# Scores of two banks in one visit, and three rotating product banks, in a sliding-window attention block

## The chip, the cores and the metric

The kernel runs on one core of a Trainium2 chip. The metric is device time in microseconds (us) of one launch, lower is better. Times before are the median of three runs. One further execution was profiled, and every row below comes from its trace. PE is TensorE with its matrix multiplications, DVE is VectorE, ACT is ScalarE, POOL is GpSimd, SP is SyncE, which issues nearly all DMAs here. A "slot" below is the place ahead of one dense matmul.

## The reference

A transformer block on 2048 tokens of width 1024, in bfloat16: layer norm, attention with 32 heads of width 32 in which each query sees the 256 keys up to itself, a residual, a second layer norm, and a dense SiLU layer of width 3584 with a residual.

```python
qkv = (layernorm(x) @ wqkv).reshape(B, S, 3, 32, 32)
scores = einsum("bhqd,bhkd->bhqk", q, k) * 32 ** -0.5
mask = (idx[:, None] - idx[None, :] >= 0) & (idx[:, None] - idx[None, :] < 256)
p = softmax(where(mask, scores, -1e9))
h = x + einsum("bhqk,bhkd->bhqd", p, v).reshape(B, S, D) @ wo
out = h + silu(layernorm(h) @ w1) @ w2
```

## The kernel before

**Tiling.** Tokens go in `NB` = 4 blocks of 512, heads in `G` = 8 groups of four. Scores have the keys on the partitions and the queries along the row, so that their exponentials are used directly as weights of the product with the values; one extra column of ones in `v` (width `VW` = 33) gives the sum for the softmax. A score matmul contracts over 32 rows. Four heads sit on four row strips of the PE array and, where the keys are taken in halves of 64, two halves on two column strips: eight tiles stream at once.

**Dense work and what is put in between.** Attention is not a stage of its own. Dense matmuls of 512 columns come in groups of eight (`v_group`, `qk_group`, `wo_group`), each group into one bank of the eight that PE can write, which DVE then copies or adds out. Each dense matmul first calls `between`, and there `Stream.between` puts pieces of the attention of the block before. Block 0's attention lies between the projections of block 1, block 1's between those of block 2, block 2's between those of block 3, and block 3's between the first 24 groups of the output projection (`dense` list with `wo_group`). Each of these stretches has 192 dense matmuls. After them come the SiLU layers (`h1_group`, `mm2`), which take up the last pieces.

**Scores.** For blocks 1 to 3 each pair of groups has five bursts: one C burst (`scores_c`, the corner parts of both groups, 16 matmuls of 128 columns) and an X and a Y burst for each group (`scores_xy`, 24 matmuls of 320, 128 and 64 columns: 512 columns for each tile). A burst fills `sc[0]` and `sc[1]`, two tiles of two banks each, one bank a head. ACT then writes the exponentials into `c_ring` or a buffer of `xy_ring`: two instructions of 1024 elements after a C burst, and 768, 256, 768, 256 after an X or Y burst. POOL masks the triangles (`select`, four of 512 elements after an X or Y burst). Block 0 has two bursts a group (`scores_0`).

**Products.** `attn_out` multiplies the exponentials with the values: per group 16 outputs of three matmuls of 33 columns. The outputs of two heads fill a bank of `o_ps`; `o_ps[0]` and `o_ps[1]` take turns. `attn_norm` (DVE: reciprocal, then a multiply into `obuf`) follows each half of a group. After a group's second half `attn_transpose` is put on the list `late`, and SP issues it ahead of the next dense group. The pieces (`SPLIT`: 8, 8, 5, 6 and 5 outputs) run just before a burst, three bursts behind their own.

**Other queues.** DVE also has the layer norm steps of the next block (`ln1_steps`, `ln2_steps`): one step after a dense group, behind the group's own copy. In block 2's stretch these are four statistics steps (groups 1, 2, 4 and 5), four short ones and four normalizations. In the output-projection stretch the second layer norm's steps begin after group 11, and from group 14 on two follow each group.

**Banks.** Eight: `acc0` and `acc1` for dense groups, `o_ps0` and `o_ps1`, and four for `sc`. In the SiLU layers the four of `sc` become `hacc`, and six banks rotate.

Of the kernel before, what the change touches and what calls it, by code (L numbers as in the profile page):

```python
# [9 lines left out]
F32 = mybir.dt.float32  # L10
# [4 lines left out]
P = 128  # L15
# [25 lines left out]
SPLIT = [(0, 8), (8, 16), (16, 21), (21, 27), (27, 32)]  # L41
# [7 lines left out]
def kernel(  # L49
# [46 lines left out]
    o_ps = [ps.tile([P, 8, 64], F32, name=f"o_ps{i}") for i in range(2)]  # L96
    acc_ps = [ps.tile([P, 512], F32, name=f"acc{i}") for i in range(2)]
# [29 lines left out]
    xy_ring = [r_e[:, 3072 + 1280 * i:3072 + 1280 * (i + 1)] for i in range(8)]  # L127
# [46 lines left out]
    def busy(n):  # L174
        nc.tensor.matmul(o_ps[0][:].rearrange("p (a c) b -> p a (c b)", c=2)[:, 0:n], lhsT=warm, rhs=wide[:, 0:n], start=True, stop=True)
# [53 lines left out]
    acc_banks = list(a[:] for a in acc_ps)  # L229
# [50 lines left out]
    def chunk_of(i, bank, piece, pair, hh):  # L280
        if bank == "C":
            return c_ring[:, (i + 1) % 3, pair * 2 + hh, piece * P:(piece + 1) * P]
        if i < G:
            c0 = hh * 512 + piece * P
        else:
            c0 = 1024 + hh * P if piece == 2 else hh * 512 + (piece - piece // 3) * P
        return xy_ring[(i % 2 * 2 + "XY".index(bank)) * 2 + pair][:, c0:c0 + P]

    def scores_xy(b, g, odd):
        q0 = odd * P  # L290
        mid, first, last = odd, odd - 2, odd + 2

        parts = [
            (mid, 0, q0, q0 + 320, 64), (mid, 1, q0 + 64, q0 + 384, 128),
            (last, 0, q0 + 256, q0 + 384, 384), (first, 1, q0, q0 + 128, 0),
            (first, 0, q0, q0 + 64, 0), (last, 1, q0 + 320, q0 + 384, 448),
        ]
        for step in range(3):
            for hh in range(4):
                for kt, half, qa, qb, col in parts[step * 2:step * 2 + 2]:  # L300
                    r0 = hh * DH
                    t = b * 4 + kt
                    k0 = (t % 4) * P + half * 64
                    nc.tensor.matmul(  # L304
                        sc[hh // 2][half * 64:half * 64 + 64, hh % 2, col:col + qb - qa],
                        lhsT=kT[t // 4][r0:r0 + DH, g, k0:k0 + 64],
                        rhs=qT[b][r0:r0 + DH, g, qa:qb],
                        start=True, stop=True, tile_position=(r0, half * 64),
                    )
        for pair in range(2):  # L310
            e = xy_ring[((b * G + g) % 2 * 2 + odd) * 2 + pair]
            tri = e[:, 0:1024].rearrange("p (h c q) -> p h c q", h=2, q=256)
            bank = sc[pair]
            both = bank[:, :, 0:192]
            both = bass.AP(tensor=both.tensor, offset=both.offset, ap=[*both.ap[:2], [320, 2], both.ap[2]])
            nc.scalar.activation(out=tri[:, :, :, 64:256], in_=both, func=ACT.Exp, scale=scale)  # L316
            nc.scalar.activation(out=e[:, 1024:1280].rearrange("p (h q) -> p h q", q=P), in_=bank[:, :, 192:320], func=ACT.Exp, scale=scale)  # L317
            four = e[:, 0:1024].rearrange("p (c q) -> p c q", q=256)
            select(four[:, :, 0:P], four[:, :, 64:64 + P], False)
            select(four[:, :, P:2 * P], four[:, :, P:2 * P], True)  # L320

    def scores_c(b, g):
        s0, s1 = (b * G + g + 1) % 3, (b * G + g + 2) % 3
        order = (g, g + 1) if s0 < s1 else (g + 1, g)
        for n, gg in enumerate(order):
            for m, (kt, q) in enumerate(((-1, 0), (2, 3))):
                t = b * 4 + kt
                for hh in range(4):
                    r0 = hh * DH
                    nc.tensor.matmul(  # L330
                        sc[hh // 2][:, hh % 2, (n * 2 + m) * P:(n * 2 + m + 1) * P],
                        lhsT=kT[t // 4][r0:r0 + DH, gg, (t % 4) * P:(t % 4 + 1) * P],
                        rhs=qT[b][r0:r0 + DH, gg, q * P:(q + 1) * P],
                        start=True, stop=True, tile_position=(r0, 0),
                    )
        lo, hi = min(s0, s1), max(s0, s1)
        for pair in range(2):
            nc.scalar.activation(out=c_ring[:, lo:hi + 1:hi - lo, pair * 2:pair * 2 + 2, :],
                                 in_=sc[pair].rearrange("p h (n q) -> p n h q", q=256), func=ACT.Exp, scale=scale)

    def scores_0(g, odd):
# [9 lines left out]
        for step in range(0, len(parts), 2):  # L351
            for hh in range(4):
                for t, half, qa, qb, col in parts[step:step + 2]:
                    r0 = hh * DH
                    k0 = t * P + half * 64
                    nc.tensor.matmul(  # L356
                        sc[hh // 2][half * 64:half * 64 + 64, hh % 2, col:col + qb - qa],
                        lhsT=kT[0][r0:r0 + DH, g, k0:k0 + 64],
                        rhs=qT[0][r0:r0 + DH, g, qa:qb],
                        start=True, stop=True, tile_position=(r0, half * 64),  # L360
                    )
        for pair in range(2):
            e = xy_ring[(g % 2 * 2 + odd) * 2 + pair][:, 0:1024].rearrange("p (h q) -> p h q", q=512)
            nc.scalar.activation(out=e[:, :, 0:256], in_=sc[pair][:, :, 0:256], func=ACT.Exp, scale=scale)  # L364
            nc.scalar.activation(out=e[:, :, 320:512], in_=sc[pair][:, :, 256:448], func=ACT.Exp, scale=scale)
            nc.scalar.activation(out=c_ring[:, (g + 1) % 3, pair * 2:pair * 2 + 2, 128 + 64 * odd:192 + 64 * odd],
                                 in_=sc[pair][:, :, 448:512], func=ACT.Exp, scale=scale)
# [10 lines left out]
    def attn_out(b, g, first, last):  # L378
        i = b * G + g
        for n in range(first, last):  # L380
            pair, qt, hh = n // 8, n // 2 % 4, n % 2
            chunks = (CHUNKS if b else CHUNKS_0)[qt]
            for m, (kt, bank, piece) in enumerate(chunks):
                nc.tensor.matmul(  # L384
                    o_ps[pair][:, qt * 2 + hh, 0:VW],
                    lhsT=chunk_of(i, bank, piece, pair, hh),
# [6 lines left out]
    def attn_norm(i, pair):  # L393
        recip = small.tile([P, 8, 1], F32, name="recip", tag="recip")
        nc.vector.reciprocal(out=recip[:], in_=o_ps[pair][:, :, DH:VW])
        nc.vector.tensor_tensor(
            out=obuf[i % 3][:, :, pair * 64:(pair + 1) * 64].rearrange("p t (h d) -> p t h d", d=DH),
            in0=o_ps[pair][:, :, 0:DH].rearrange("p (t h) d -> p t h d", h=2),
# [8 lines left out]
    def attn_piece(b, g, first, last):  # L407

        for k in range(2):
            a, z = max(first - 16 * k, 0), min(last - 16 * k, 16)  # L410
            if a < z:
                attn_out(b, g + k, a, z)
                if z == 16:
                    late.append(lambda k=k: attn_transpose(b, g + k))

    class Stream:

        def __init__(self, b):  # L420
            self.bursts, self.pieces, self.done, self.seen = [], [], 0, 0
            self.behind = 3 if b else 2
            pending.extend(coming)
            coming.clear()
            for g in range(0, G, 2):
                if b:
                    self.bursts += [lambda g=g: scores_c(b, g)]
# [365 lines left out]
```

## Time and profile before

| | |
|---|---|
| median of three runs | 690.07 us (689.61 to 691.45) |
| the profiled execution | 689.68 us |
| its span, first to last instruction | 688.0 us |
| granted TensorE clock | 1.00 of full speed |

The time by stretch of the span, from the view that sums each engine's busy time in windows:

| stretch, us | what | PE busy, us | DVE | ACT | POOL |
|---|---|---|---|---|---|
| 0 to 48.0 | start, projections of block 0 | 46.70 | 23.58 | 20.25 | 2.97 |
| 48.0 to 102.9 | block 0's attention among block 1's projections | 54.90 | 34.05 | 35.07 | 37.39 |
| 102.9 to 289.0 | attention of blocks 1 to 3 | 186.10 | 102.47 | 123.59 | 120.78 |

In time lines a row has the start and the length in us, the engine, the line of the kernel, the operation, the tile written and the tiles read, the shape and how many instructions were merged; in brackets stands how long the engine was idle before and what ended that. PE's matmuls are pipelined: the listed length of one is longer than the distance to the next, so distances between starts are what count.

### The profile page before, as it was taken

What the parts mean: (1) busy time and instruction counts of PE and PEld (TensorE: products, weight loads), DVE (VectorE), ACT (ScalarE), POOL (GpSimd) and SP (SyncE); (2) the same over time, 40 slices, a digit from 0 to 9 for tenths busy, and PEclk for the clock granted to TensorE, in tenths of its full rate; (3) what the DMA queues carried; (4) which work ended last, traced back from release to release, by engine and by line L of the source; (5) the groups of instructions that cost most, each with busy time, mean ns of one, the idle gap of its engine ahead of it and who ended that gap; (6) DMA issues with size and microseconds to landing.
All of it is one profiled execution on the core that took longest, in us unless ns stands there. A gap on an engine that the chain in (4) does not pass through costs nothing.

```text
span 688.0 us, 14237 instructions
## 1 busy us (share of the span) xinstructions
PE 684.0 (99%) x6008; PEld 342.4 (50%) x6008; DVE 292.0 (42%) x614; ACT 244.6 (36%) x462; POOL 161.1 (23%) x295
## 2 busy tenths in 40 slices
PE   9999999999999999999999999999999999999998
PEld 4445555555555555544444444444444444444445
DVE  5268647744444459433316133342233251333111
ACT  7326667667666766421300033200133100233000
POOL 1016765576666657400000000000000000000000
DMA  8741241136241986891023310023300123100010
GB/s 280 255 74 59 47 95 41 33 55 186 74 129 34 299 246 186 177 318 58 15 93 107 85 39 0 1 91 75 80 0 1 30 88 90 39 1 1 30 39 24
DMA packets 77616, 61.48 MB, mean 89 GB/s; under 512 B 52464, under 2 KB 60656, under 8 KB 77552
## 3 DMA queue, kind: packets, MB, share of 16 engines
q1 hardware_dynamic: 77408, 60.31, 31.5%
q8 instruction: 47, 0.77, 0.5%
q10 hardware_dynamic: 144, 0.26, 0.1%
q14 instruction: 17, 0.14, 0.1%
HBM read 39.85 MB, written 8.39 MB: 70 GB/s over the span
## 4 chain that ended last, share of the span: by engine, by line
PE 99%; DMA 0%; DVE 0%; issue 0%; DVEq 0%
PE hacc L703 20%; PE acc L251 17%; PE hacc L740 15%; PE acc L740 14%; PE acc L703 9%; PE acc L272 7%; PE acc L241 7%; PE o_ps L384 5%; PE sc L304 3%; PE hacc L272 2%; PE sc L356 1%; PE sc L330 1%; PE acc L523 1%; PE o_ps L523 1%; PE tp L241 1%; DMA r_o<-in_A_x_dram 0%
## 5 line engine op out<-in xcount | busy, mean ns | idle before, releaser
L374 POOL TENSOR_SCALAR_AFFINE_SELECT r_e<-r_e 128x512 bf16<-128x512 bf16 (+1 forms) x288 | 158.2, 564 | 122.6 <-ACT r_e L364 59.7
L740 PEld LDWEIGHTS <-r_a 128*128 128x128 bf16 x952 | 90.9, 98 | 103.0
L703 PEld LDWEIGHTS <-r_w 128*128 128x128 bf16 x896 | 87.4, 98 | 104.8
L703 PE MATMUL hacc<-r_e,r_w 128*128 128x512 bf16 x480 | 106.0, 379 | 0.0
L740 PE MATMUL hacc<-r_a 128*128 128x512 bf16 (+1 forms) x504 | 100.6, 361 | 0.0
L316 ACT ACTIVATE r_e<-sc 128x768 bf16<-128x768 f32 x96 | 78.1, 814 | 47.6 <-PE sc L304 46.7
L740 PE MATMUL acc<-r_a 128*128 128x512 bf16 (+1 forms) x448 | 95.0, 372 | 0.0
L712 ACT ACTIVATE r_n<-hacc 128x512 f32<-128x512 f32 x30 | 17.9, 597 | 178.9 <-PE hacc L703 178.9
L251 PEld LDWEIGHTS <-r_w 128*128 128x128 bf16 x512 | 47.2, 98 | 55.0 <-issue 1.0
L253 DVE CAST r_a<-acc 128x512 bf16<-128x512 f32 x56 | 38.7, 692 | 56.8 <-PE acc L251 56.5
L251 PE MATMUL acc<-r_t,r_w 128*128 128x512 bf16 x256 | 59.6, 380 | 0.0
L251 PE MATMUL acc<-r_w 128*128 128x512 bf16 x256 | 57.8, 380 | 0.0
L384 PEld LDWEIGHTS <-r_e 128*128 128x128 bf16 x1440 | 47.4, 96 | 17.9
L272 PE MATMUL acc<-r_o,r_a 128*128 128x512 bf16 x208 | 48.7, 380 | 0.0
L384 PE MATMUL o_ps<-r_a,r_e 128*128 128x33 bf16 x1440 | 48.1, 178 | 0.0
L703 PE MATMUL acc<-r_e,r_w 128*128 128x512 bf16 x192 | 43.4, 379 | 0.0
L755 DVE SCALAR_TENSOR_TENSOR r_t<-acc,r_t 128x512 bf16<-128x512 f32 (+1 forms) x16 | 10.6, 665 | 69.3 <-PE acc L740 69.3
L317 ACT ACTIVATE r_e<-sc 128x256 bf16<-128x256 f32 x96 | 37.4, 390 | 0.0
L272 PEld LDWEIGHTS <-r_a 128*128 128x128 bf16 x256 | 23.4, 98 | 27.0
L713 DVE SCALAR_TENSOR_TENSOR r_a<-r_n,hacc 128x512 bf16<-128x512 f32 x30 | 20.6, 688 | 33.0 <-ACT r_n L712 33.0
L713 DVE SCALAR_TENSOR_TENSOR r_a<-r_a,hacc 128x512 bf16<-128x512 f32 x30 | 20.6, 688 | 31.2 <-ACT r_a L712 31.2
L755 DVE SCALAR_TENSOR_TENSOR r_t<-hacc,r_t 128x512 bf16<-128x512 f32 (+1 forms) x18 | 11.6, 647 | 50.3 <-PE hacc L740 50.3
(106 smaller groups left out, 552.7 us busy)
## 6 DMA issues: line engine op xcount, KB each, us to landing
r_w<-in_B_w_dram SPq DMA_DIRECT2D x8, 896.0 KB, 6.2
r_a<-in_B_w_dram SPq DMA_DIRECT2D x7, 1024.0 KB, 7.7
r_w<-in_A_wqkv_dram SPq DMA_DIRECT2D x4, 1024.0 KB, 9.4
h_dram<-r_t SPq DMA_DIRECT2D x16, 256.0 KB, 3.6
r_t<-h_dram SPq DMA_DIRECT2D x16, 256.0 KB, 2.8
out_dram<-r_t SPq DMA_DIRECT2D x31, 128.0 KB, 1.7
r_e<-h_dram SPq DMA_DIRECT2D x3, 1024.0 KB, 6.0
r_o<-in_A_x_dram SPq DMA_DIRECT2D x11, 256.0 KB, 4.9
```

Source lines behind the costliest of these rows:

```text
L241: nc.tensor.matmul(acc, lhsT=lnT_b[b % 2][:, kt, j * P:(j + 1) * P], rhs=wv[:, kt, c * 512:(c + 1) * 512], start=(kt == 0), stop=(kt == KT ...
L251: nc.tensor.matmul(acc, lhsT=wqk[:, kt, col0:col0 + P], rhs=lnT_b[b % 2][:, kt, :], start=(kt == 0), stop=(kt == KT - 1))
L253: copy(out=(qT, kT)[which][b][:, g, :], in_=acc)
L272: nc.tensor.matmul(acc, lhsT=qT[b][:, g, j * P:(j + 1) * P], rhs=wo[:, g, c * 512:(c + 1) * 512], start=(g == 0), stop=(g == G - 1))
L316: nc.scalar.activation(out=tri[:, :, :, 64:256], in_=both, func=ACT.Exp, scale=scale)
L317: nc.scalar.activation(out=e[:, 1024:1280].rearrange("p (h q) -> p h q", q=P), in_=bank[:, :, 192:320], func=ACT.Exp, scale=scale)
L374: nc.gpsimd.affine_select(out=dst, in_=src, pattern=[[0, n] for n in dst.shape[1:-1]] + [[sgn, P]], compare_op=ALU.is_ge if upper else ALU ...
L384: nc.tensor.matmul(o_ps[pair][:, qt * 2 + hh, 0:VW], lhsT=chunk_of(i, bank, piece, pair, hh), rhs=v[:, b * 4 + kt, g * 4 + pair * 2 + hh, ...
L703: nc.tensor.matmul(acc, lhsT=w1[:, kt, ft * P:(ft + 1) * P], rhs=ln2T[b][:, kt, :], start=(kt == 0), stop=(kt == KT - 1))
L713: nc.vector.scalar_tensor_tensor(out=gT[:, ft, :], in0=th, scalar=1.0, in1=acc, op0=ALU.add, op1=ALU.mult)
L740: nc.tensor.matmul(acc[:, 0:c1 - c0], lhsT=gT[:, ft, j * P:(j + 1) * P], rhs=w2[ft // 4][:, ft % 4, c0:c1], start=(ft == 0), stop=(ft == F ...
L755: nc.vector.scalar_tensor_tensor(out=t_out[j % 2][:, c0:c1], in0=acc[:, 0:c1 - c0], scalar=0.5, in1=t_in[j % 2][:, c0:c1], op0=ALU.mult, o ...
```

## The change

Scores of blocks 1 to 3 are made in three visits per pair of groups, 36 in all, where there were five bursts, 60 in all. A pair has 20 bank-fulls of scores (4 heads times C, X, Y of the first group and X, Y of the second). A visit makes one bank-full for all four heads in `sc` ("own") and a second bank-full for two or three of them ("more") in banks that belong to others:

- first visit: X of the first group, and C of heads 0, 1, 2;
- second visit: Y of the first group, C of head 3, and X of the second group for heads 0 and 1;
- third visit: Y of the second group, and its X for heads 2 and 3.

The banks are now four separate tensors: three rotate for dense groups, the fourth (`o_ps`) is for products. In a visit `idle` is the one that the next dense group will write, `behind` the one that the group before has just left, `out` the products' bank. Visits stand at slots 4, 20 and 36 of each 48, that is with four matmuls of the current group still to come. The products of a group are two pieces of 24 matmuls, at slots 42, 47, 58 and 63 after the pair's beginning, no longer next to a burst; their one bank takes both halves in turn. C is computed in halves of 64 keys like X and Y. `sc` is one tensor of four banks. Buffers hold all four heads of X or Y. Block 0 keeps its bursts and pieces (`First`). In the SiLU layers seven banks rotate.

```diff
-    o_ps = [ps.tile([P, 8, 64], F32, name=f"o_ps{i}") for i in range(2)]
-    acc_ps = [ps.tile([P, 512], F32, name=f"acc{i}") for i in range(2)]
+    four = [ps.tile([P, 512], F32, name=f"bank{i}") for i in range(4)]
+    o_ps = four[3].rearrange("p (a b) -> p a b", b=64)
...
+    def exp_xy(e, banks, h0, h1):
+        tri, mid = banks[:, :, 0:192], banks[:, :, 192:320]
+        tri = bass.AP(tensor=tri.tensor, offset=tri.offset, ap=[*tri.ap[:2], [320, 2], tri.ap[2]])
+        nc.scalar.activation(out=tri_of(e)[:, h0:h1, :, 64:256], in_=tri, func=ACT.Exp, scale=scale)
+        nc.scalar.activation(out=full_of(e)[:, h0:h1, :], in_=mid, func=ACT.Exp, scale=scale)
...
+    def visit(i, n):
+        now = acc_n[0] % 3
+        idle, behind, out = (now + 1) % 3, (now + 2) % 3, 3
+        if n == 0:
+            own, e_own = unit_xy(i, 0), xbuf(i)
+            more = [(0, idle, unit_c(i)), (1, out, unit_c(i)), (2, behind, unit_c(i))]
+        elif n == 1:
+            own, e_own = unit_xy(i, 1), ybuf(i)
+            more = [(3, idle, unit_c(i)), (0, behind, unit_xy(i + 1, 0)), (1, out, unit_xy(i + 1, 0))]
+        else:
+            own, e_own = unit_xy(i + 1, 1), ybuf(i + 1)
+            more = [(2, out, unit_xy(i + 1, 0)), (3, behind, unit_xy(i + 1, 0))]
+        todo = []
+        for h in range(4):
+            for half in range(2):
+                runs = [(sc[:, h, :], own[half])]
+                for hh, bank, unit in more:
+                    if hh == h:
+                        runs.append((four[bank], unit[half]))
+                at = 0
+                for bank, parts in runs:
+                    for p in parts:
+                        todo.append((at, h, half, bank, p))
+                        at += p[3] - p[2]
+        todo.sort(key=lambda m: m[0])
+        for _, h, half, bank, (ii, kt, qa, qb, col) in todo:
...
+        side = [h for h, _, unit in more if len(unit[0]) == 3]
+        for h, bank, unit in more:
+            if h in side:
+                exp_xy(xbuf(i + 1), four[bank].rearrange("p (h q) -> p h q", h=1), h, h + 1)
+            else:
+                exp_c(i, h, bank)
+        if side:
+            select_xy(xbuf(i + 1), side[0] // 2)
+        exp_xy(e_own, sc[:], 0, 4)
+        for pair in range(2):
+            select_xy(e_own, pair)
...
+    class Stream:
+        def __init__(self, left):
+            self.seen = 0
+            self.visits, self.pieces = {}, {0: left[0], 10: left[1], 15: left[2]}
+            for p in range((NB - 1) * G // 2):
+                i, t = G + 2 * p, 48 * p + 4
+                for n in range(3):
+                    self.visits[t + 16 * n] = (i, n)
+                for n in range(4):
+                    self.pieces[t + (38, 43, 54, 59)[n]] = (i + n // 2, n % 2)
+
+        def between(self, kt):
+            if self.seen in self.pieces:
+                attn_piece(*self.pieces.pop(self.seen))
+            if self.seen in self.visits:
+                visit(*self.visits.pop(self.seen))
+            self.seen += 1
...
-    sc = [sc_pool.tile([P, 2, 512], F32, name=f"sc{i}") for i in range(2)]
+    sc = sc_pool.tile([P, 4, 512], F32, name="sc")
```

The matmuls of a visit are put in the order of the column at which they stand in their head's two banks (`todo.sort`), so the first bank-full of all heads comes first. The exponentials follow in the order of `more`, then `sc`: 512 elements for a C of one head, 384 and 128 for an X of one head, 1536 and 512 for the four heads in `sc`.

More of the change, by code (lines that the diff above doesn't have):

```diff
@@ L228 @@
     acc_n = [0]
-    acc_banks = list(a[:] for a in acc_ps)
+    acc_banks = [b[:] for b in four]
     def next_acc():
@@ L322, in scores_c @@
[L322 to L339, printed above, removed]
+        return [
+            [(i, mid, q0, q0 + 320, 64), (i, last, q0 + 256, q0 + 384, 384), (i, first, q0, q0 + 64, 0)],
+            [(i, mid, q0 + 64, q0 + 384, 128), (i, first, q0, q0 + 128, 0), (i, last, q0 + 320, q0 + 384, 448)],
+        ]
@@ L687 @@
                 steps.pop(0)()
-    pending += coming
+    pending = [lambda piece=piece: attn_piece(*piece) for piece in stream.rest()]
     while steps:
```

147 lines of the change are left out of this document (67 added, 80 removed).

## The prediction

> **What bounds the kernel now.** I read the page first (busy shares, then the chain of work that ended last), then the time line of the attention stretch engine by engine, then single waits.
>
> ```profile
> PE 684.0 (99%) x6008; PEld 342.4 (50%) x6008; DVE 292.0 (42%) x614; ACT 244.6 (36%) x462; POOL 161.1 (23%) x295
> ...
> PE 99%; DMA 0%; DVE 0%; issue 0%; DVEq 0%
> ```
>
> PE sets the time alone: nobody makes it wait, so the change can win only by taking PE work out, and loses whatever wait it puts in. Next, PE alone in the attention stretch (start, length, line, operation, count):
>
> ```profile
> 173.32 1.24 PE L241 MATMUL acc<-r_w,r_t 128*128 128x512 bf16 x5
> 174.40 0.76 PE L384 MATMUL o_ps<-r_a,r_e 128*128 128x33 bf16 x24
> 175.09 0.43 PE L304 MATMUL sc<-r_a 32*64 32x320 bf16 x24
> 175.45 2.12 PE L241 MATMUL acc<-r_w,r_t 128*128 128x512 bf16 x9
> 177.40 0.76 PE L384 MATMUL o_ps<-r_a,r_e 128*128 128x33 bf16 x24
> 178.09 0.40 PE L330 MATMUL sc<-r_a 32*128 32x128 bf16 x16
> 178.42 0.39 PE L241 MATMUL acc<-r_w,r_t 128*128 128x512 bf16 x1
> ```
>
> Lengths overlap, so I go by starts. Five dense matmuls take 174.40 - 173.32 = 1.08, 0.216 each, 0.42 ns a column. Twenty-four product matmuls and the step into the scores take 0.69. An X or Y burst, from its first matmul to the next dense one, takes 0.36; a C burst 0.33.
>
> ```profile
> 46.26 1.67 PE L251 MATMUL acc<-r_w 128*128 128x512 bf16 x7
> 47.86 0.37 PE L356 MATMUL sc<-r_a 32*64 32x320 bf16 x8
> ```
>
> ```profile
> 284.35 0.76 PE L384 MATMUL o_ps<-r_a,r_e 128*128 128x33 bf16 x24
> 284.95 0.38 PE L703 MATMUL acc<-r_a,r_w 128*128 128x512 bf16 x1
> ```
>
> From dense work straight into scores: 1.60 - 7 x 0.216 = 0.09 lost. Products followed by dense work: 0.60 for 24, 0.025 each and nothing lost. So products into scores cost 0.69 - 0.60 = 0.09 - hardly less than dense into scores - and products by themselves cost no turn.
>
> **The PE work.** In a burst each of the eight tiles (four heads by two halves) streams 320 + 128 + 64 = 512 columns, 0.216; the rest of 0.36 is fixed. A visit gives three heads (in the third visit two) another 512 columns behind the first, so by the column rate it takes 0.36 + 0.22 = 0.58. Per pair of groups before: 4 x 0.36 + 0.33 + 5 x 0.085 = 2.19. After: 3 x (0.58 + 0.09) = 2.01. That is -0.18 a pair, -2.2 us over 12 pairs. The 192 further score matmuls (C now in halves) lie in tiles that stream side by side. Bounds: columns must stream, so a second run is no cheaper than 0.22; at worst it costs a whole burst, 0.36, which is 36 x 0.14 = 5.0 more (sum +2.8). I take the low end: inside a burst the later steps already follow the first at the column rate.
>
> Block 0 keeps its 16 bursts and its product order; the products keep their 1,440 matmuls. Free as well: the 16 selects a pair (POOL is 23% busy; a product piece comes 22 dense matmuls, over 4.7 us, after its scores, and ACT's 3.5 plus two selects have about a microsecond to spare there; were they a microsecond late, 12 us), and the 32 transposes on SP's queue, issued as before when the next group begins, with a buffer that is reused three groups later.
>
> **The waits.** All banks were spare before. Now a visit writes into two product banks and the one for attention products. Rows of the other engines around the burst above:
>
> ```profile
> 175.20 0.21 DVE L395 RECIPROCAL recip<-o_ps 128x8 f32<-128x8 f32 x1 [1.42 <-PE o_ps L384]
> 175.44 0.42 DVE L396 TENSOR_TENSOR r_n<-o_ps,recip 128x256 bf16<-128x256 f32 x1
> ...
> 175.68 0.81 ACT L316 ACTIVATE r_e<-sc 128x768 bf16<-128x768 f32 x1 [0.88 <-PE sc L304]
> 175.88 0.70 DVE L243 CAST r_a<-acc 128x512 bf16<-128x512 f32 x1
> ...
> 178.59 1.94 ACT L338 ACTIVATE r_e<-sc 128x1024 bf16<-128x1024 f32 x2 [0.84 <-PE sc L330]
> ```
>
> ```profile
> 4.41 0.31 DVE L479 TENSOR_SCALAR r_e<-r_o,mean 128x128 bf16<-128x128 bf16 x1
> ...
> 4.78 0.23 PE L483 MATMUL tp<-ident,r_e 128*128 128x128 bf16 x1 [0.18 <-DVE r_e L479]
> ```
>
> A released PE starts 0.06 after the releasing instruction's end (4.72 to 4.78). I use that for ACT too.
>
> *W1, the bank behind, first and second visit.* That bank holds the previous group's product, which DVE copies out. In that group a product piece ends one dense matmul before the group does, so DVE has the piece's normalization first. Clock from the piece's last matmul: reciprocal at 0.22 (174.40 + 23 x 0.025 = 174.98 to 175.20), multiply at 0.46, copy 0.34 later (rows below: 119.97 to 120.31) at 0.80, done 1.49, PE free to write at 1.55. PE wants it after one dense matmul of the old group (starts at 0.025), four of the new (the visit begins 5 x 0.216 + 0.09 later, at 1.20), and the first 512 columns (0.24): 1.44. Behind the waiting matmul stand the rest of the visit, and behind that ACT. Stall 0.1, 24 times: 2.4. Bounds: 0, if the rows' rounding and an earlier release take it away, to 0.25, where the copy would wait for the multiply's full 0.42 and the reciprocal comes later: 0 to 6. The third visit follows a group without pieces: no stall.
>
> *W2, the score bank, third visit.* Only 16 dense matmuls lie between second and third visit: from PE's return to dense work 16 x 0.216 + 0.09 = 3.55. In that time ACT must empty what the second visit left: one 512, twice (384 and 128), one 1536, one 512. Start to start:
>
> ```profile
> 48.33 0.60 ACT L364 ACTIVATE r_e<-sc 128x512 bf16<-128x512 f32 x1 [1.50 <-PE sc L356]
> 48.82 0.48 ACT L365 ACTIVATE r_e<-sc 128x384 bf16<-128x384 f32 x1
> 49.19 0.28 ACT L366 ACTIVATE r_e<-sc 128x128 bf16<-128x128 f32 x1
> 49.35 0.62 ACT L364 ACTIVATE r_e<-sc 128x512 bf16<-128x512 f32 x1
> ```
>
> So 512 costs 0.49, 384 0.37, 128 0.16. Two 1024 end after 1.94 where one lasts 1.02: 0.92 each. 1536 is not in the trace; by the step from 512 to 1024 it is 0.92 + 0.43 = 1.35. ACT begins 0.17 after PE returns (178.42 to 178.59). Sum: 0.17 + 0.49 + 2 x 0.53 + 1.35 + 0.62 (full length, it is last) + 0.06 = 3.75, against 3.55: stall 0.2, 12 times, 2.4. Bounds: 0 to 0.87 (no overlap between exponentials, rival C). The other deadlines hold narrowly: the idle bank is read first, 0.17 + 0.60 + 0.06 = 0.83 after PE returns, and wanted after four dense matmuls, 0.86; it would cost 24 times its overrun.
>
> The Trainium skill (ScalarE: Activation LUTs, What ACT_TABLE_LOAD costs) gives an activation as 186 ns plus 0.833 ns an element with only 93 ns of overlap back to back. The rows show 0.11 to 0.12 of overlap. By the Trainium skill's figures the chain would be 4.29 - 0.56 + 0.23 = 3.96, W2 0.41, 4.9 in all, and the time 2.5 later, an estimate; the rows decide here.
>
> *W3, layer norm steps in DVE's queue.* One bank now takes both halves' products, so the second piece (five dense matmuls after the first) waits until DVE has normalized the first. Before, two banks took turns and this was hidden. Where a statistics step is queued ahead:
>
> ```profile
> 117.79 0.64 DVE L243 CAST r_a<-acc 128x512 bf16<-128x512 f32 x1
> 118.34 1.28 DVE L182 BATCH_NORM_STATS2 ln_st<-r_o 128x6 f32<-128x512 bf16 x2
> 119.66 0.21 DVE L190 BATCH_NORM_AGGREGATE st_a<-ln_st 128x2 f32<-128x12 f32 x1
> 119.78 0.15 DVE L395 RECIPROCAL recip<-o_ps 128x8 f32<-128x8 f32 x1
> 119.97 0.42 DVE L396 TENSOR_TENSOR r_n<-o_ps,recip 128x256 bf16<-128x256 f32 x1
> 120.31 0.68 DVE L243 CAST r_a<-acc 128x512 bf16<-128x512 f32 x1
> ```
>
> ```profile
> 254.01 0.69 DVE L182 BATCH_NORM_STATS2 ln_st<-r_a 128x6 f32<-128x512 bf16 x1 [0.56 <-DMA r_a<-h_dram]
> ```
>
> From the last dense matmul of the group before: copy at 0.43 (175.45 to 175.88), statistics 0.6 later, reciprocal 1.44 after them, multiply 0.2 after that, 0.42 long, 0.06: 3.15. PE is at the second piece after 8 x 0.216 + 0.61 = 2.34. Stall 0.8 where group 4 of block 2 (a statistics group) precedes the piece group 5. In the output-projection stage the first statistics step stands behind a load, 0.56 in the row; with W1 its addition starts at 0.77, statistics at 0.77 + 0.69 + 0.56 = 2.02, next addition 3.46, second statistics 4.06, reciprocal 5.5, bank free 6.18; PE comes at 16 x 0.216 + 0.77 + 0.61 = 4.84: 1.3. Then from group 14 two steps a group: I put 0.6 each at the third visit in group 16 and the pieces in group 17, less than one statistics step's 0.8. W3: 3.3; bounds 1 (the load early, short steps hidden) to 6.
>
> Sum: -2.2 + 2.4 + 2.4 + 3.3 = +5.9. The profiled execution took 689.68 (its span 688.0 and 1.7 around it), so 695.6; the median of the runs shown lies 0.4 above that execution.
>
> **Rivals.**
>
> A, not slower: a release reaches PE 0.2 earlier than the profiled end of the instruction, because its tail (the 0.1 by which rows overlap) isn't waited for. It decides from 0.1 for W1 and 0.2 for W2, which both vanish; W3's four become 2.5: +0.3, 690.0. For: consecutive rows overlap on both engines. Against: the 0.06 row, after the full end. Chance 0.11.
>
> B, faster: no wait is met at all, the layer norm steps falling between pieces: -2.2, 687.5. PE never waits today, but today nothing is asked of it within 1.5 us. Chance 0.06.
>
> C, much slower: ACT doesn't overlap single-head exponentials. Second-visit chain 0.60 + 2 x 0.76 + 1.45 + 0.62 + 0.23 = 4.42, W2 0.87, 10.4 in place of 2.4: 703.6. Against: the four rows. Chance 0.07.
>
> D, the change doesn't do what it says: a visit's second run costs a whole burst, +5.0: 700.6. For: matmuls issue in order, so a head that waits holds the others. Against: 24 matmuls take 0.36. Chance 0.10.
>
> **How the numbers follow.** Forecast 0.66, with a range of its own of 692.5 to 699. What a measurement here can tell from no change is 0.3%, 2.1 us, so the bounds are 688.0 and 692.1. Faster: B and a little of A, 0.07. Same: most of A and the forecast's low tail, 0.12. Slower: 0.81. The range 690.5 to 701 takes in A's edge and D, and leaves out B, C and tails.
>
> **What would show it.** PE should list waits for the first time: about 24 in score matmuls behind DVE's copies (0.1 each), 12 behind ACT's last exponential (0.2), and three or four of 0.5 to 1.5 behind DVE in the products or a visit, near 118, 262 and 270. A visit with no wait from first score to dense should take 0.58, each entry 0.09. If PE lists no wait, B or A stands and the prediction is wrong; if visits take 0.72, D; if W2 is near 0.9, C.

## The result, and the profile after

The changed kernel takes 696.45 us, median of four runs (695.68 to 696.66), against 689.88 for the kernel before: 1.0088 times as long, 95% interval 1.0071 to 1.0106. The profiled execution took 696.58, its span 694.9, at a granted clock of 1.00. The span is 6.9 longer than before; the forecast made it 5.9.

The page of the changed kernel, busy shares and the chain that ended last:

```profile
PE 676.7 (97%) x6084; PEld 340.4 (49%) x6200; DVE 290.2 (42%) x614; ACT 241.9 (35%) x462; POOL 160.8 (23%) x295
...
PE 89%; ACT 5%; issue 2%; DVE 2%; DMA 1%; POOL 0%; ACTq 0%; DVEq 0%
```

PE was 99% of the chain and is 89%; ACT, DVE and a DMA now stand in it. (PE issued 6,200 weight loads but the trace holds 6,084 matmuls: records of dense matmuls are missing, so a row below can count one too few, and its length is then no guide; distances between starts hold.)

The view of PE's waits, with the total, the number and the longest:

```profile
PE bank L421 <- DVE r_n L433: 2.9, 3, 1.5
...
PE bank L360 <- DVE r_t L285: 1.0, 1, 1.0
```

These are the long waits that the forecast put behind layer norm steps: three in the products (line 421), one in a visit (line 360). The short ones don't show here and have to be read from starts. PE's time line around a second and a third visit, and around a first one:

```profile
171.06 0.43 PE L360 MATMUL sc<-r_a 32*64 32x320 bf16 x24
171.40 0.42 PE L360 MATMUL bank<-r_a 32*64 32x320 bf16 x20
171.76 3.63 PE L252 MATMUL bank<-r_w,r_t 128*128 128x512 bf16 x15
175.46 0.43 PE L360 MATMUL sc<-r_a 32*64 32x320 bf16 x24
```

```profile
226.45 0.43 PE L360 MATMUL sc<-r_a 32*64 32x320 bf16 x24
226.69 0.50 PE L360 MATMUL bank<-r_a 32*64 32x128 bf16 x24
227.12 1.47 PE L283 MATMUL bank<-r_o,r_a 128*128 128x512 bf16 x5
```

The second visit starts its second run 171.40 - 171.06 = 0.34 in, the first visit 0.24: the second waits 0.1 for a bank. From PE's return to dense work at 171.76, sixteen dense matmuls (one record is missing) end at 171.76 + 16 x 0.216 = 175.22, and the third visit starts at 175.46: 0.24, of which 0.09 is the turn into scores and 0.15 a wait. Over all visits, from starts to the nanosecond: first 0.68 us, second 0.69, third 0.58; third visits begin 0.15 to 0.18 late, the others on time. What the third visit waits for is ACT's last exponential of a second visit. PE's return to dense work behind one and the third visit that follows, and ACT's rows between them:

```profile
109.95 0.61 PE L252 MATMUL bank<-r_w 128*128 128x512 bf16 x2
...
113.69 0.43 PE L360 MATMUL sc<-r_a 32*64 32x320 bf16 x24
```

```profile
110.10 0.60 ACT L315 ACTIVATE r_e<-bank 128x512 bf16<-128x512 f32 x1 [1.78 <-PE bank L360]
110.59 0.49 ACT L321 ACTIVATE r_e<-bank 128x384 bf16<-128x384 f32 x1
110.96 0.28 ACT L322 ACTIVATE r_e<-bank 128x128 bf16<-128x128 f32 x1
111.12 0.51 ACT L321 ACTIVATE r_e<-bank 128x384 bf16<-128x384 f32 x1
111.49 0.31 ACT L322 ACTIVATE r_e<-bank 128x128 bf16<-128x128 f32 x1
111.65 1.50 ACT L321 ACTIVATE r_e<-sc 128x1536 bf16<-128x1536 f32 x1
112.98 0.66 ACT L322 ACTIVATE r_e<-sc 128x512 bf16<-128x512 f32 x1
```

It ends at 112.98 + 0.66 = 113.64, and the next score matmul starts at 113.69: the 0.05 from release to PE that the forecast took from another place.

The largest wait, near 262. PE's products and DVE's queue:

```profile
258.86 0.76 PE L421 MATMUL bank<-r_a,r_e 128*128 128x33 bf16 x24
259.47 1.24 PE L283 MATMUL bank<-r_o,r_a 128*128 128x512 bf16 x5
262.16 0.77 PE L421 MATMUL bank<-r_a,r_e 128*128 128x33 bf16 x24 [1.45 <-DVE r_n L433]
```

```profile
257.94 1.29 DVE L193 BATCH_NORM_STATS2 ln_st<-r_a 128x6 f32<-128x512 bf16 x2 [0.78 <-DMA r_a<-h_dram]
259.27 0.21 DVE L201 BATCH_NORM_AGGREGATE st_b<-ln_st 128x2 f32<-128x12 f32 x1
259.44 0.69 DVE L285 TENSOR_TENSOR r_t<-bank,r_a 128x512 bf16<-128x512 f32 x1
260.05 1.28 DVE L193 BATCH_NORM_STATS2 ln_st<-r_a 128x6 f32<-128x512 bf16 x2
261.36 0.21 DVE L201 BATCH_NORM_AGGREGATE st_b<-ln_st 128x2 f32<-128x12 f32 x1
261.49 0.16 DVE L432 RECIPROCAL recip<-bank 128x8 f32<-128x8 f32 x1
261.68 0.42 DVE L433 TENSOR_TENSOR r_n<-bank,recip 128x256 bf16<-128x256 f32 x1
```

PE is ready for the second piece at 259.47 + 5 x 0.216 = 260.55 and starts it at 262.16, 1.61 later. The first piece was done by 259.5, but DVE normalizes it only at 261.49: it stood 0.78 behind the load of the row, then took a statistics step, an addition and another statistics step. Read in the same way, 0.87 is lost near 118, 0.09 near 133, 0.87 near 274, and 1.29 in the visit near 270. W3 is 4.7 in all.

### The profile page after: what moved, and what is told of

The parts are those of the page before. It is cut to its first block, busy times and chain, and to the rows that moved or that the text cites. A ratio compares the mean times of both kernels' runs of the same rounds, so it can differ in the third digit from the quotient of the medians.

```text
span 694.9 us, 14583 instructions
## 1 busy us (share of the span) xinstructions
PE 676.7 (97%) x6084; PEld 340.4 (49%) x6200; DVE 290.2 (42%) x614; ACT 241.9 (35%) x462; POOL 160.8 (23%) x295
## 4 chain that ended last, share of the span: by engine, by line
PE 89%; ACT 5%; issue 2%; DVE 2%; DMA 1%; POOL 0%; ACTq 0%; DVEq 0%
PE hacc L783 16%; PE hacc L746 16%; PE bank L262 13%; PE bank L746 12%; PE bank L783 12%; PE bank L252 5%; PE bank L421 5%; PE bank L283 4%; ACT r_e L321 4%; PE sc L360 2%; PE bank L360 2%; ACT r_e L322 1%; PE bank L566 1%; PE hacc L283 1%; PE sc L392 1%
## 5 line engine op out<-in xcount | busy, mean ns | idle before, releaser
L783 PE MATMUL hacc<-r_a 128*128 128x512 bf16 (+2 forms) x550 | 114.0, 366 | 0.5
L783 PE MATMUL bank<-r_a 128*128 128x512 bf16 (+1 forms) x386 | 81.0, 368 | 0.4
L264 DVE CAST r_a<-bank 128x512 bf16<-128x512 f32 x56 | 38.6, 689 | 61.8 <-PE bank L262 48.3
L746 PE MATMUL bank<-r_e,r_w 128*128 128x512 bf16 x282 | 63.6, 379 | 0.3
L262 PE MATMUL bank<-r_t,r_w 128*128 128x512 bf16 x233 | 56.4, 379 | 2.3 <-issue 1.6
L262 PE MATMUL bank<-r_w 128*128 128x512 bf16 x240 | 55.9, 379 | 1.4 <-issue 0.8
L321 ACT ACTIVATE r_e<-sc 128x1536 bf16<-128x1536 f32 x36 | 53.5, 1485 | 0.0
L283 PE MATMUL bank<-r_o,r_a 128*128 128x512 bf16 x201 | 49.8, 379 | 2.0 <-issue 1.1
L421 PE MATMUL bank<-r_a,r_e 128*128 128x33 bf16 x1440 | 46.2, 178 | 2.9 <-DVE r_n L433 2.9
L252 PE MATMUL bank<-r_w,r_t 128*128 128x512 bf16 x116 | 28.3, 379 | 1.2 <-issue 0.8
```

The costliest lines, as they stand in the source:

```text
L252: nc.tensor.matmul(acc, lhsT=lnT_b[b % 2][:, kt, j * P:(j + 1) * P], rhs=wv[:, kt, c * 512:(c + 1) * 512], start=(kt == 0), stop=(kt == KT ...
L262: nc.tensor.matmul(acc, lhsT=wqk[:, kt, col0:col0 + P], rhs=lnT_b[b % 2][:, kt, :], start=(kt == 0), stop=(kt == KT - 1))
L264: copy(out=(qT, kT)[which][b][:, g, :], in_=acc)
L283: nc.tensor.matmul(acc, lhsT=qT[b][:, g, j * P:(j + 1) * P], rhs=wo[:, g, c * 512:(c + 1) * 512], start=(g == 0), stop=(g == G - 1))
L321: nc.scalar.activation(out=tri_of(e)[:, h0:h1, :, 64:256], in_=tri, func=ACT.Exp, scale=scale)
L421: nc.tensor.matmul(o_ps[:, qt * 2 + hh, 0:VW], lhsT=chunk_of(i, bank, piece, pair * 2 + hh), rhs=v[:, b * 4 + kt, g * 4 + pair * 2 + hh, : ...
```

## The experiments

All were timed beside the kernel before, which took 690.20 in the first group of runs, 690.34 in the second and 690.45 in the last. The changed kernel itself was not timed again, so its 696.45 stands against these only to some tenths of a microsecond.

**One part at a time.** Each of the three waits was taken away alone, and then all three. W2, by one dense matmul more ahead of the third visit:

```diff
-                    self.visits[t + 16 * n] = (i, n)
+                    self.visits[t + (0, 16, 33)[n]] = (i, n)
```

> Third visit one dense matmul later in its group, nothing else. Theory T (the loss is a sum of separate waits with a price each): the 12 waits on ACT before the third visit, 0.15 to 0.18 each in the changed kernel's trace, vanish, since PE comes 0.22 later; about -2.0 us against the changed kernel's span of 694.9, so 692.9. Rival R (DVE and ACT are short of time as a whole, so a wait taken away at one place comes back at the next deadline): the same ACT work is waited for elsewhere, less than 1 us is gained. Rival U (the loss is PE's own, visits and turns that cost more than bursts): no gain.

W1 of first visits, by earlier pieces:

```diff
-                    self.pieces[t + (38, 43, 54, 59)[n]] = (i + n // 2, n % 2)
+                    self.pieces[t + (37, 42, 54, 59)[n]] = (i + n // 2, n % 2)
```

> The two product pieces of a pair's first group one dense matmul earlier (37 and 42 after the pair's first visit in place of 38 and 43); the second group's stay. Theory T: the normalization then ends 0.22 earlier against the first visit that follows, and the 0.1 wait on DVE's copy in that visit goes, 12 x 0.1 = -1.2 us, less some 0.05 at each earlier piece where the product bank's exponentials come late, and 0.2 more behind each of three layer norm steps: -0.4 to -1.0, and the 12 second visits keep their 0.11. R and U: no gain; R expects that the second visits or the pieces wait more by the same amount.

W3, by statistics, short steps and normalizations behind other groups:

```diff
-            if steps and n >= 1 and n != 3:
-                steps.pop(0)()
-            elif turns and n % 3 == 2:
+            if steps:
+                for _ in range({1: 1, 2: 1, 5: 1, 7: 1, 8: 2, 9: 2, 11: 1, 13: 1, 14: 1, 15: 1}.get(n, 0)):
+                    steps.pop(0)()
+            elif turns and n % 2 == 1:
...
-        for _ in range(1 if n < 14 else 2):
-            if steps and n >= 11:
-                steps.pop(0)()
+        for _ in range({11: 1, 13: 1, 14: 1, 15: 2, 17: 2, 19: 2, 20: 4, 21: 3}.get(n, 0)):
+            steps.pop(0)()
```

> The layer norm steps in DVE's queue run behind groups that no product piece follows in the next group (none behind groups 4, 6, 10, 12, 16, 18, 22 of a stretch), the same steps otherwise. Theory T: the four long waits near 118, 262, 270 and 274 (0.87, 1.6, 1.3 and 0.87) shrink to at most 1 together: -3.5 us, span 691.4; W1 and W2 stay as they are. R: the steps are then in the way of the copies, and what is won at the pieces is lost in the visits. U: no gain.

> The three edits together. Theory T: the prices add, -2.0 - 0.7 - 3.5 = -6.2 us, span 688.7, about the time of the kernel before; what is left are some 12 waits of 0.1 in second visits, and 1 to 2 of single waits, so the PE work itself would be 2 shorter than before. R: less than half of it. U: as the changed kernel, 694.9.

Measured: 698.04, 698.26, 696.56, and 694.29 for all three (ratios 1.0113, 1.0117, 1.0090 and 1.0058, each within 0.0016). None of the single edits made it faster, and all three together won 2.2 us, not the 6.2 of theory T. Yet two of the waits went as the theory says: with the third visit later all twelve third visits start without delay, and with the pieces earlier all twelve first visits take 0.65 and not 0.68. The gain was taken back further on. The products and DVE's queue of the kernel with the third visit later:

```profile
257.76 1.24 PE L283 MATMUL bank<-r_o,r_a 128*128 128x512 bf16 x5
261.71 0.85 PE L421 MATMUL bank<-r_a,r_e 128*128 128x33 bf16 x24 [2.71 <-DVE r_n L433]
```

```profile
257.31 1.29 DVE L193 BATCH_NORM_STATS2 ln_st<-r_a 128x6 f32<-128x512 bf16 x2 [1.85 <-DMA r_a<-h_dram]
```

PE comes to this place 1.7 us earlier (257.76 against 259.47), but DVE gets its row only 0.6 earlier (257.31 against 257.94), so the wait near 262 grows from 1.6 to 2.9. Behind this wait the granted clock of the profiled execution fell to 0.50 from 262 to 266 and 0.78 from 266 to 270, and the seventeen dense matmuls between second and third visit, with the entry, took 4.79 there (265.63 to 270.42) in place of 3.77. That is a loss of its own; but the one execution at a clock of 1.00 took 696.94, so the gain of 2.0 was gone without it too. With the pieces earlier, three of the product waits (near 118, 133 and 274) grew by just the 0.2 by which the piece came sooner, since what ends them is DVE's queue and not the piece; the one near 262 grew by 0.34. Moving the norm steps removed the waits near 118 and 270, but those near 262 and 274 stayed at 1.49 and 0.73, one of 0.8 came up in a third visit near 129, and the SiLU layers began 1.3 late, behind the last transposes. That pointed to the load behind group 9, which has a time of its own and pins the stretch behind it.

**The load, and W3 with it.** Only the output-projection stretch is changed: each row is loaded by itself, two groups after its store, and its steps are spread.

```diff
-        if n == 9:
-            steps = ln2_steps(0)
-            steps.pop(0)()
+        if n in (4, 6, 8, 10):
+            j = n // 2 - 2
+            nc.sync.dma_start(out=h_blk[0][:, j, :], in_=h_dram[j * P:(j + 1) * P, :])
+        if n == 4:
+            steps = ln2_steps(0)[1:]
...
-        for _ in range(1 if n < 14 else 2):
-            if steps and n >= 11:
-                steps.pop(0)()
+        for _ in range({7: 1, 8: 1, 11: 1, 13: 1, 14: 1, 15: 2, 17: 2, 19: 2, 20: 2, 21: 3}.get(n, 0)):
+            steps.pop(0)()
```

> Only the layer norm steps of the output-projection stage are moved: each of the four rows is loaded by itself two groups after its store (groups 4, 6, 8, 10), in place of all four in one load at group 9, and the steps are queued behind groups that no product piece follows. Theory D (the long waits of this stage are made by DVE standing in its queue, first behind the late load, then behind two steps a group): the waits of 1.62 near 262, 1.29 in the visit near 270 and 0.87 near 274 go, the one of 0.87 near 118 stays, nothing new above 0.3: 696.4 - 3.8 = 692.6 (692 to 693.5). Rival B (the one bank for both pieces is what is short, whatever DVE does beside it): the waits come back in other groups of the stage, 695.5 or more.

Measured: 694.34 (694.26 to 694.64), 2.1 less than the changed kernel. PE's waits, all that are left in this view beside one in the start:

```profile
PE bank L747 <- DMA r_a<-r_a: 0.7, 1, 0.7
PE bank L421 <- DVE r_n L433: 0.7, 1, 0.7
```

The waits near 262 and 270 are gone and the one near 274 is 0.26: 3.5 of W3 was DVE's queue in this stretch, as theory D has it. But the SiLU layers, the next in line, now wait for the last transposes, 0.7 in the view and 0.9 from starts, and the end of the span comes 0.25 later behind the last matmul (2.88 against 2.64). That leaves 2.35 of the 3.5; the span gained 2.3.

**W2, both ways.** On this kernel, where the late load no longer swallows a gain, the third visit is put one dense matmul later, `(0, 16, 33)`, and one earlier, `(0, 16, 31)`.

> ln2_by_rows (694.34) with the third visit one dense matmul later. Theory W2 (a third visit waits 0.15 to 0.18 for ACT's last exponential of the second visit): one dense matmul more between the two is 0.216, so all twelve waits go and 2.0 us with them, since the stage that swallowed this gain in third_later no longer waits for its load: 692.3. Rival G (PE's gain is given back to the next wait, as in third_later, where nothing was left): 694 or more.

> ln2_by_rows (694.34) with the third visit one dense matmul earlier. Theory W2: the twelve waits grow by one dense matmul each, 0.216, from 0.165 to 0.38, 2.6 us: 696.9. Rival C2 (the long entry of a third visit is the turn into a visit of two heads, not a wait for ACT): no change, 694.3.

Measured: 692.89 and 696.37, against 694.34. One later, every third visit starts without delay, and 1.45 of the 2.0 comes through: a product wait of 0.86 near 255 is new and the one near 133 grew by 0.15, while the SiLU layers wait 0.3 less. One earlier, the delays are 0.36 to 0.39, larger by 0.21 to 0.22 each; the view of waits now names them (the time was 2.0 longer and not 2.6, since the SiLU layers waited 0.7 less):

```profile
PE sc L360 <- ACT r_e L322: 3.7, 12, 0.3
```

So W2 is a wait for ACT's chain, worth one for one what PE brings forward, and rival C2 is out.

**W1, and what a visit needs by itself.** Both pairs of pieces one dense matmul earlier:

```diff
-                    self.pieces[t + (38, 43, 54, 59)[n]] = (i + n // 2, n % 2)
+                    self.pieces[t + (37, 42, 54, 58)[n]] = (i + n // 2, n % 2)
```

> Both piece pairs come one dense matmul earlier where a visit follows (37, 42, 54, 58 in place of 38, 43, 54, 59). Theory S (the trace of after: a first visit needs 0.65 us by itself and only 0.03 of its 0.68 is a wait; a second visit starts its second run 0.09 late, which is the wait for the bank behind, and needs 0.60 by itself): the second visits go from 0.69 to 0.60, the first from 0.68 to 0.65, 12 x 0.115 = 1.4 us less; the second piece now comes sooner behind the first, so product waits of 0.05 to 0.1 appear 12 times and the three long ones near 118, 262 and 274 grow by 0.2 each, together 1.2 to 1.8 more: 696.2 to 697. Theory W (my prediction: every visit needs 0.58 and what lies above it is a wait): both visits go to 0.58, 2.5 us less and the same 1.2 to 1.8 more: 695.2 to 695.8. The lengths of the visits decide, not the time.

Measured: 697.75. The second visits went from 0.69 to 0.585 (eleven of twelve; the first lies behind block 0's pieces, which weren't moved), the first visits from 0.68 to 0.65, each to 2 ns. Neither theory had both right: second visits need 0.58, as predicted, first visits 0.65. W1 was 12 x 0.107 + 12 x 0.028 = 1.6. The time did not fall, because new product waits of 0.11 to 0.17 came up ten times, 1.25 in all, and the four old ones grew, by another 1.2. Theory S expected both, but only 1.2 to 1.8 for the two together. Whether the first visit's further 0.07 comes from the number of matmuls was tried by taking C in whole tiles of 128 keys, half as many matmuls:

```diff
-                        todo.append((at, h, half, bank, p))
+                        if len(parts) == 3 or half == 0:
+                            todo.append((at, h, half, bank, (*p, 3 - len(parts))))
...
+            n_keys = 128 if whole else 64
             nc.tensor.matmul(
-                bank[half * 64:half * 64 + 64, col:col + qb - qa],
-                lhsT=kT[t // 4][r0:r0 + DH, g, k0:k0 + 64], rhs=qT[b][r0:r0 + DH, g, qa:qb],
+                bank[half * 64:half * 64 + n_keys, col:col + qb - qa],
+                lhsT=kT[t // 4][r0:r0 + DH, g, k0:k0 + n_keys], rhs=qT[b][r0:r0 + DH, g, qa:qb],
```

> In a visit the C scores are taken with all 128 keys of a tile in one matmul (32x128 tiles) in place of two halves, so a first visit has 36 matmuls, not 48, a second 40, not 44, a third 36 as before. Theory N (a visit is lengthened by each matmul beyond 36, 0.0057 us): first visits 0.58 to 0.60 in place of 0.65 to 0.68, second 0.67 in place of 0.69: 1.0 us less, 695.4. Rival M (PE must drain before it takes tiles of another shape, as it does between dense work and scores, 0.09): 24 turns of 0.09 more, 2.2 us, visits 0.74 and 0.75: 698.6.

Measured: 702.12. A first and a second visit of this kernel, each with the dense work behind it:

```profile
136.55 0.43 PE L362 MATMUL sc<-r_a 32*64 32x320 bf16 x24
136.91 0.40 PE L362 MATMUL bank<-r_a 32*128 32x128 bf16 x12
137.24 1.47 PE L262 MATMUL bank<-r_w 128*128 128x512 bf16 x6
...
142.02 0.43 PE L362 MATMUL sc<-r_a 32*64 32x320 bf16 x24
142.36 1.09 PE L362 MATMUL bank<-r_a 32*64 32x320 bf16 x16
143.38 3.63 PE L262 MATMUL bank<-r_w 128*128 128x512 bf16 x16
```

Theory N is out. In a first visit, which turns once from 32x64 to 32x128 tiles, the second run starts 0.36 in and not 0.24, and the visit takes 0.69 in spite of twelve matmuls fewer. A second visit, where the order by column alternates between the two shapes, takes 143.38 - 142.02 = 1.36, 0.67 more. By the starts of its single matmuls it changes the shape four times, and less the columns of the step ahead these changes take 0.12, 0.09, 0.12 and 0.10: 0.43 of the 0.67. The rest is put down to columns of the two shapes that no longer stream side by side, which nothing tried alone. Rival M has the mechanism right, but not the sizes: its 0.74 was too high for first visits, and its 0.75 far too low for second ones, for which it counted one turn. The Trainium skill (TensorEngine Tiling (Array Packing), Key Properties) says that a change of the tiling mode drains the engine. The runs agree: 0.09 to 0.12 is what it costs here. So whole tiles gain nothing in first visits (0.69 against 0.65 to 0.68) and lose 0.67 in each second one.

The number of matmuls alone doesn't explain the 0.07, since a second visit with eight more than a third needs no longer. The starts of single matmuls in best_try, the last run below, where first visits don't wait, tell more. The last matmul of a first visit starts 0.503 in, that of a second or third visit 0.464 in; and dense work follows a first visit's last matmul 0.147 behind its start, a second's 0.121. C's last step has 128 columns and X's has 64, and 64 columns are 0.027; the bursts of the kernel before show the same two figures, 0.147 behind C and 0.120 behind X or Y. So 0.03 of the 0.07 is the longer last step, and 0.04 a later start: from the second of C's four steps on, most matmuls start about 0.008 apart, as their weight loads do, where those of the steps ahead start 0.003 apart. That the weight loads set this pace is likely, but no run tried it.

**All of it.** Third visit later, pieces at 37, 42, 54 and 58, the norm steps of the block stretches moved, and the rows loaded singly.

> Third visit one dense matmul later, pieces at 37, 42, 54, 58, layer norm steps of the attention stages behind groups that no piece follows, and the rows of the output-projection stage loaded singly. Theory S (waits 7.0 to 8.0 above what the visits themselves need; the scores' own work is only 12 x 0.08 = 1.0 us less than before): all of W1, W2 and W3 but 1 us go, 689.0 (688.3 to 690), no different from the kernel before (690.2). Theory W (the visits themselves need 0.58 each, 2.2 us less than before): 687.8. Rival R (waits move on to the next resource, as in the runs with single edits): 692 or more.

Measured: 692.64, 1.0033 times the kernel before (1.0021 to 1.0046). All visits but two are at their own length, as theory S has them; the time is rival R's. Left are eleven product waits of 0.12, one of 0.08, one of 0.26, 0.72 in a third visit near 129 and, from starts, 1.25 ahead of the SiLU layers. The last try moves the second piece of a pair's second group behind the end of the dense group and spreads the norm steps once more:

```diff
-                    self.pieces[t + (38, 43, 54, 59)[n]] = (i + n // 2, n % 2)
+                    self.pieces[t + (37, 42, 54, 60)[n]] = (i + n // 2, n % 2)
...
+                for _ in range({2: 1, 3: 1, 5: 1, 8: 1, 9: 1, 11: 1, 14: 2, 15: 2, 17: 2}.get(n, 0)):
...
+        for _ in range({8: 1, 9: 1, 11: 1, 14: 1, 15: 2, 17: 3, 20: 7}.get(n, 0)):
```

> All edits together, with the last piece behind the end of its group (37, 42, 54, 60), and the layer norm steps behind groups that no piece and no visit follows at once, few at a time. Theory S (what is left of the change when nothing waits: visits of 0.65, 0.58 and 0.58 and three entries of 0.09 against five bursts and entries before, 0.11 a pair, 1.3 us in all): every visit at its own length, product waits under 0.1, 0.5 to 1 us left where the output-projection stage ends: 689.5 to 690.5, no different from the kernel before (690.3). Rival R (another wait takes the place of those removed): 692 or more. A version that is faster than the kernel before by more than 0.3% would need waits of less than nothing: under 688.2 both are wrong.

Measured: 692.02 (691.5 to 692.77, eleven runs), 1.0024 times the kernel before (1.0015 to 1.0033). Its visits, and all its waits beside the one in the start:

```profile
149.57 0.43 PE L360 MATMUL sc<-r_a 32*64 32x320 bf16 x24
149.81 0.47 PE L360 MATMUL bank<-r_a 32*64 32x128 bf16 x24
150.22 1.47 PE L262 MATMUL bank<-r_w 128*128 128x512 bf16 x6
...
154.99 0.43 PE L360 MATMUL sc<-r_a 32*64 32x320 bf16 x24
155.23 0.41 PE L360 MATMUL bank<-r_a 32*64 32x320 bf16 x20
155.57 3.84 PE L262 MATMUL bank<-r_w 128*128 128x512 bf16 x17
159.35 0.43 PE L360 MATMUL sc<-r_a 32*64 32x320 bf16 x24
159.60 0.39 PE L360 MATMUL bank<-r_a 32*64 32x320 bf16 x12
159.93 1.04 PE L262 MATMUL bank<-r_w 128*128 128x512 bf16 x4
```

```profile
PE bank L748 <- issue: 1.1, 1, 1.1
PE bank L360 <- DVE r_t L285: 0.5, 1, 0.5
PE bank L360 <- DVE r_a L264: 0.2, 1, 0.2
```

The three kinds of visit take 150.22 - 149.57 = 0.65, 0.58 and 0.58. Read from starts, 1.28 is still lost ahead of the SiLU layers, 0.83 and 0.54 in two third visits, 0.21 in one product and 0.11 in a second visit: 3.0, where 0.5 to 1 was expected. Its span of 690.3 without these would be 687.3, 0.7 under the span before. So even with every wait gone the change would win less than a measurement here can tell from nothing. That last step is worked out and was not run.

## Why the prediction was right, and where its terms were not

The time (696.45 against 695.6) and the sign were right, and so was the cause: PE's own work falls little, and waits that weren't there before outweigh it. By its own terms, in us, measured from starts:

| term | predicted | measured | shown by |
|---|---|---|---|
| PE work | -2.2 | -1.1 | lengths of the visits that don't wait |
| W1, bank behind | 2.4 | 1.6 | both pairs of pieces earlier |
| W2, score bank | 2.4 | 2.0 | third visit one later, one earlier |
| W3, layer norm steps | 3.3 | 4.7 | rows loaded singly, norm steps moved |
| sum | 5.9 | 7.2, span 6.9 | |

PE work and W3 cost more than predicted, by 1.1 and 1.4, W1 and W2 less, by 0.8 and 0.4. That the sum came within a microsecond of the span is in part luck.

*PE work.* The visit of 0.58 by the column rate holds for second and third visits to the hundredth, and so does the entry of 0.09, which puts rival D out. The first visit needs 0.65. With 0.09 for each entry that is 0.65 + 0.585 + 0.58 + 0.28 = 2.10 a pair against 2.19, 0.09 less and not 0.18. The step that failed is that the 192 further C matmuls lie free beside others: their last step of 128 columns costs 0.03 a first visit, their later starts 0.04.

*W1.* Place, cause and size were right for second visits (0.11 against 0.1), and too large for first visits, 0.03. The wait is there too: by single starts head 2's first C matmul comes 0.338 in where it comes 0.257 in without a wait. But the last one comes only 0.03 later than without, 0.532 for 0.503, since without the wait the matmuls behind it start one at a time. The two errors, 1.1 and 0.8, stood against each other: the first visits' 0.68 was at first sight a wait of 0.1, as predicted, and only the run without the wait showed it to be work.

*W2.* The chain was put at 3.75 from PE's return to dense work. In the rows shown it is 109.95 to 113.69, 3.73 to the nanosecond. The 1536 exponential takes 1.50 (mean 1.485), and the next starts 1.33 behind it, where 1.35 was put. PE's own side, sixteen dense matmuls and the entry, takes 3.56, so that 0.175 is left here. By the Trainium skill (ScalarE: Activation LUTs, What ACT_TABLE_LOAD costs) the chain would have been 3.96 and the wait 0.41, an estimate; the trace does not agree with its 93 ns of overlap, since successive exponentials start 0.11 to 0.17 before the one ahead ends.

*W3.* This is the mis-sized term. The mechanism is shown by the rows near 262 and by the run that moves those steps away. The sizes: 0.87 for 0.8 near 118; 1.6 for 1.3 near 262, mostly because the load held DVE 0.78 and not 0.56; 1.29 for 0.6 in the third visit near 270, and 0.87 for 0.6 near 274. I had put 0.6 for each of the last two because two short steps would take less than a statistics step. DVE's queue ahead of the visit near 270:

```profile
266.38 1.28 DVE L193 BATCH_NORM_STATS2 ln_st<-r_a 128x6 f32<-128x512 bf16 x2
...
267.93 0.60 DVE L209 TENSOR_SCALAR ln_var<-st_b 128x4 f32<-128x4 f32 x1
268.56 0.17 DVE L210 TENSOR_SCALAR rs_b<-ln_var 128x4 int32<-128x4 int32 x1
268.77 0.48 DVE L211 TENSOR_SCALAR rs_b<-rs_b 128x4 int32<-128x4 int32 x1
269.16 0.68 DVE L285 TENSOR_TENSOR r_t<-bank,r_a 128x512 bf16<-128x512 f32 x1
```

The two steps of group 14 are not two short ones: the last statistics take 1.5, and the short step behind them is three instructions that take 1.3 (267.93 to 269.25) on 4 numbers a row. Together they hold the addition of group 15 until 269.16, and PE, whose visit needs that bank, until 269.89. I had counted steps and not looked at what they issue.

Nor had I looked at POOL, whose selects the prediction called free. Two of these three instructions began while a select ran:

```profile
267.87 2.65 POOL L411 TENSOR_SCALAR_AFFINE_SELECT r_e<-r_e 128x512 bf16<-128x512 bf16 x4 [0.18 <-ACT r_e L321]
```

The first of the four selects ends at 268.51 and the second at 269.23; the DVE instructions end 0.02 later, at 268.53 and 269.25, after 0.60 and 0.48 where the one between them took 0.17. That is 0.74 more than three times 0.17. Less this, the wait near 270 would be 0.55, close to the 0.6 put. Another, 0.48 in place of 0.16, stands in the queue ahead of the wait near 274. So the larger part of what this term lacked is what the selects do to DVE. This is read from rows: no run moved the selects.

*Rivals.* A and B want no waits: out. C wants third visits 0.87 late: out, 0.15 to 0.18. D wants visits of 0.72: out.

## What to carry to other kernels

When a kernel's critical engine never waits, its spare buffers are what keeps it so: taking them for fewer, larger bursts pays only if the work saved is larger than one wait per burst, and both are tenths of a microsecond here. A wait that is removed alone may win nothing, because a transfer with a time of its own pins the next one; look for the last thing in the stretch that has a fixed time, and move that first. An instruction that is short in one place can be several times as long in another: take its length from where it will stand, with the other engines at work. A visit that is longer than its columns isn't waiting until a run without the wait has shown its own length.

## What the runs showed of the hardware

A change of the tile's shape within scores, between 32x64 and 32x128, costs 0.09 to 0.12 us of PE, about as much as the 0.09 between dense work and scores; in an order that alternates it made one visit 0.67 longer, with four changes. Dense work starts 0.147 behind the start of a last score step of 128 columns and 0.120 behind one of 64. DVE's arithmetic on four numbers a row (lines 209 to 216) mostly took 0.15 to 0.21, and up to 0.65 in places. In the thirteen traces together 192 of these instructions took over 0.24: each began while a POOL select ran and ended within 0.03 of that select's end. Of the 848 that began with no select running, none took so long; 52 others began under a select and were not held. In one trace (third_later) PE's granted clock fell to 0.50 for 6.8 us around the end of an idle time of 2.7; the waits of up to 2.0 in the other traces had no such fall. It is one case, and no run tried it. Block 0's first score matmul starts between 47.97 and 48.74 us in the traces of kernels that are alike up to there: up to 0.8 us of a single profiled execution is the start's own.
